# Cap first on SyncE's queue, and pair 7's normalization and the third weight unit's decoding moved to other places

## The chip, the cores and the metric

The kernel runs on one core of a Trainium2 chip. The core has five engines that run side by side, each its own list of instructions in a fixed order: TensorE (PE, with its weight loads as PEld), VectorE (DVE), ScalarE (ACT), GpSimd (POOL) and SyncE (SP), which only issues DMAs here. An instruction that needs another engine's result waits on a semaphore, and all that stands behind it on its own engine waits too. The metric is the device time of one execution in microseconds (us), as the median of several runs; less is better.

## The reference

Attention with capped scores, then a first feed-forward layer, then a gated one behind an RMS norm. All is float32.

```python
def _attn_ref(q, k, v, cap):                      # 2 x 12 heads, 448 tokens, 64 each
    scores = np.matmul(q, k.transpose(0, 1, 3, 2)) / np.sqrt(64)
    scores = cap * np.tanh(scores / cap)
    attn = np.exp(scores - np.max(scores, axis=-1, keepdims=True))
    attn = attn / (np.sum(attn, axis=-1, keepdims=True) + 1e-09)
    return np.matmul(attn, v)

x = attention, as (896, 768)
h = x @ w_in                                      # 768 x 2048
x = (h * (1.0 / (1.0 + np.exp(-1.702 * h)))) @ w_out
xn = x / np.sqrt(np.mean(x * x, axis=-1, keepdims=True) + 1e-06) * rms_g
g, val = xn @ w_gate, xn @ w_val                  # 768 x 1536 each
return (g * (1.0 / (1.0 + np.exp(-g))) * val) @ w_out2
```

## The kernel before

**Attention.** The 24 heads are taken as 12 pairs (p = 0 to 11), one head on each half of the 128 partitions. The 448 keys of a head are three chunks of 128 and one of 64. For each chunk PE multiplies keys with queries (scores, line 246, and scores_last, line 273), and ACT takes the tanh (line 292, line 262 for the first chunk of pair 0, in two halves) and then the exponential (line 295). The tanh needs `tsc`, 1 / (8 cap), which DVE works out from `capt` (lines 216 and 217), a DMA that spreads the one number cap over 128 partitions. The probabilities of chunks 0 and 1 lie in `pa`, those of chunk 2 and of the short chunk in `pb`. PE multiplies them with v (outputs, line 314), and copy_out moves the result to `z`.

**The sums below the fraction.** For pair p, add_two (line 333) adds chunks 0 and 1 on DVE into `ts`. add_third adds a further part: for pair 11 DVE adds chunk 2 (line 337), for pairs 1 to 9 two DMAs add the short chunk, for pairs 0 and 10 nothing is added. sums (line 356) then sums over the keys on PE by multiplying with ones: `ts`, then chunk 2 where it isn't in `ts`, then the short chunk where it isn't. DVE transposes the result, takes the reciprocal and transposes back (lines 361, 363 and 365, the last into `rs`), and spread (line 375) sends it out in four DMAs into `r`.

**The normalization.** norm(p) is three DVE instructions: norm_mul (line 378, z times r), norm_hi (line 383, x rounded to the form that TensorE multiplies fast) and norm_lo (line 390, what the rounding left). For pairs 10 and 11 norm_hi runs on ACT (line 385). NORMS tells which pairs are normalized in which step of the loop over p; at p = 12, the last step, pairs 8 and 9 have fixed places, and pairs 10 and 11 come behind the loop and behind the first feed-forward column.

**The weights.** Every weight is split into a high and a low part, so each product is three matmuls: high with x high (line 566), high with x low (line 567), low with x high (line 568). The weights come in units of 768 columns, as raw 32-bit words that are decoded: scale (ACT, line 129), shift, top and low (DVE, lines 133, 137 and 143), high_part (ACT, line 155) and low_part (DVE, line 160). Units 0 and 1 are decoded within the attention, as the table `plan` says. Unit 2 is decoded around the end of the attention, unit 3 behind it. low(w) is the last reader of a raw buffer; there are three, so unit 5 can be loaded only behind low(2).

**The first feed-forward columns.** A column is one unit times one part of the tokens: six groups (one for each 128 rows of x) of three matmuls. Part 0 is 384 tokens, which need pairs 0 to 5 alone, part 1 is 512, which need all. The columns come in the order (unit 0, part 0), (1, 0), (0, 1), (1, 1), (2, 1), (3, 1), (2, 0), (3, 0), (4, 0) and so on. Behind a column ACT takes the gate (line 592) and rounds it (line 595), and DVE takes what is left (line 598, into `g`).

**What sets the order.** The order on every engine is that in which the code is written (manual schedule). In the feed-forward part, tick() runs a column's products first, then the work that fell due, then the decoding of that place. The list `first` behind the first column decodes unit 2 as far as that has not been done, and then unit 3 and 4; an operation that has already run is skipped. Pair 11's steps (`norm_last`) fall due just behind the first column, and ahead of that column's own gate.

Of the kernel before, what the change touches and what calls it, by code (L numbers as in the profile page):

```python
# [12 lines left out]
ALU = mybir.AluOpType  # L13
# [4 lines left out]
def attn_moe_kernel(  # L18
# [14 lines left out]
    nc = tc.nc  # L33
# [10 lines left out]
    NPR = B * NP  # L44
# [4 lines left out]
    def f(ap):  # L49
        return ap.bitcast(F32)  # L50

    keep = ctx.enter_context(tc.tile_pool(name="keep", bufs=1))
    capt = keep.tile([128, 1], F32, name="capt")
# [108 lines left out]
    def run(op, w):  # L162
        if w < len(units) and (op, w) not in done:
            done.add((op, w))
            op(w)
# [8 lines left out]
    def attention():  # L174
        with ExitStack() as actx:
# [15 lines left out]
            xs, raws, vs, pa, pb, zt, nr, ts_ = {}, {}, {}, {}, {}, {}, {}, {}  # L191
# [15 lines left out]
            cuts = [slice(0, S), slice(64, 192), slice(192, XW - S), slice(0, 64)]  # L207
# [121 lines left out]
            LAST = range(1, NPR - 2)  # L329
# [5 lines left out]
            def add_third(p):  # L335
                if p == NPR - 1:
                    nc.vector.tensor_tensor(out=ts_[p], in0=ts_[p], in1=pb[p][:, 0:2], op=ALU.add)
                elif p in LAST:
                    for j in range(2):
                        nc.gpsimd.dma_start(  # L340
                            out=ts_[p][half[j], :, j * SH:(j + 1) * SH],
                            in_=pb[p][half[j], 2].rearrange("p (e s) -> p e s", e=2), accum_op=ALU.add,
                        )

            def sums(p):
                ps = ps_s.tile([128, 2, 512], F32, tag="s", name="s")[:, 0]
                streams = [ts_[p], *([] if p == NPR - 1 else [pb[p][:, 0:2]]), *([] if p in LAST else [None])]
                for n, some in enumerate(streams):
                    for e in range(2):
                        for j in range(2):  # L350
                            if some is None:
                                w, t = blk[:, 64 * j:64 * j + 32], pb[p][:, 2, e * SH:(e + 1) * SH]
                            else:
                                w, t = f(ones)[:, 0:32], some[:, e, j * SH:(j + 1) * SH]
                            r0 = 64 * j + 32 * e
                            nc.tensor.matmul(  # L356
                                out=ps[r0:r0 + 32, 0:SH], lhsT=w, rhs=t,
                                start=(n == 0), stop=(n == len(streams) - 1), skip_group_check=True,
                            )
                by_token = zrp.tile([128, SH // 32, 32], F32, tag="bt", name="bt", bufs=2)  # L360
                nc.vector.transpose(out=by_token.rearrange("p b t -> p (b t)"), in_=ps[:, 0:SH])
                few = zrp.tile([128, SH // 32], F32, tag="few", name="few", bufs=2)
                nc.vector.reciprocal(out=few, in_=by_token[:, :, 0])
                nr[p] = zrp.tile([128, SH], F32, tag="rs", name="rs", bufs=2)
                nc.vector.transpose(  # L365
                    out=nr[p], in_=few.rearrange("p (b o) -> p b o", o=1).to_broadcast([128, SH // 32, 32]),
                )
# [9 lines left out]
            def norm_mul(p):  # L377
                nc.vector.tensor_tensor(out=zt[p], in0=zt[p], in1=nr.pop(p), op=ALU.mult)

            def norm_hi(p):  # L380
                b, pp = divmod(p, NP)
                if p < NPR - 2:
                    nc.vector.tensor_copy(xA[0][:, pp, b * S:(b + 1) * S], zt[p])
                else:
                    nc.scalar.activation(out=xA[0][:, pp, b * S:(b + 1) * S], in_=zt[p], func=AF.Copy)

            def norm_lo(p):
                b, pp = divmod(p, NP)
                xx = slice(b * S, (b + 1) * S)
                nc.vector.tensor_tensor(  # L390
                    out=xA[1][:, pp, xx], in0=zt.pop(p), in1=f(xA[0][:, pp, xx]), op=ALU.subtract
                )

            def norm(p):
                for step in (norm_mul, norm_hi, norm_lo):
                    step(p)

            nc.vector.memset(f(xA[0][:, 0, 0:S]), 1.0)
            ts = first_kq()
            nc.scalar.dma_start(out=ts[0], in_=q[0])  # L400
            nc.scalar.dma_start(out=ts[2], in_=k[0, :, cuts[2]])
            nc.scalar.activation(out=tiny, in_=f(ones)[:, 0:1], func=AF.Tanh)
            nc.sync.dma_start(out=ts[1], in_=k[0, :, cuts[1]])
            nc.sync.dma_start(out=capt, in_=cap.rearrange("(o n) -> o n", o=1).to_broadcast([128, 1]))
            nc.sync.dma_start(out=ts[3], in_=k[0, :, cuts[3]])
            constants()
            load_kq(1)
# [22 lines left out]
            scale_by_cap()  # L430

            RAW = {1: 1, 3: 2, 4: 3, 10: 4}
            NORMS = {10: (4, 5), 11: (6, 7), 12: ()}

            for p in range(NPR + 1):
                load_kq(p + 3 if p < 2 else p + 4)
                load_v(p + 2)
                if p == 1:
                    load_kq(5)
                if p in RAW:  # L440
                    load_to(RAW[p])
                if p == 0:
                    first_scores()
                    scores(0, 1)
                    tanh(0, 1)
                    exp(pa[0][:, 0])
                    scores(0, 2)
                    tanh(0, 2)
                    scores_last(0)
                    tanh(0, NC)  # L450
                    exp(pa[0][:, 1])
                    exp(pb[0])
                    outputs(0, (0,))
                    split_kq(1)
                    for c in range(NC):
                        scores(1, c)
                    outputs(0, (1,))
                elif p < NPR:
                    for c in range(NC):
                        tanh(p, c)  # L460
                subtract = cast_kq(p + 2) if p + 2 < NPR else None
                for n in NORMS.get(p, (p - 6,) if p >= 6 else ()):
                    norm(n)
                decode(p, "b")
                if subtract:
                    subtract()
                decode(p, "c")
                if p >= 1:
                    if p == NPR:
                        add_third(p - 1)  # L470
                        sums(p - 2)
                        spread(p - 2)
                    if p < NPR:
                        outputs(p - 1, (NC,))
                        scores_last(p)
                        outputs(p - 1, range(NC) if p > 1 else (2,))
                    else:
                        outputs(p - 1)
                    if p < NPR:
                        copy_out(p - 1, "D")  # L480
                    done_ = p - 1 if p == 1 or p == NPR else p - 2
                    if done_ not in nr:
                        if p == NPR:
                            norm(8)
                        sums(done_)
                        if p == NPR:
                            copy_out(p - 1, "A")
                        spread(done_)
                        if p == NPR:
                            norm(9)  # L490
                if 1 <= p < NPR:
                    tanh(p, NC)
                    exp(pa[p])
                    exp(pb[p])
                if p < NPR:
                    add_two(p)
                    decode(p, "d")
                    if p < NPR - 1:
                        add_third(p)
                if p >= 1:  # L500
                    for c in range(NC):
                        scores(p + 1, c)
            norm_mul(NPR - 2)
            norm_hi(NPR - 2)
            run(shift, 2)
            norm_lo(NPR - 2)
            q_ = NPR - 1
            return lambda: norm_mul(q_), lambda: norm_hi(q_), lambda: run(low, 2), lambda: norm_lo(q_)

    def rest(*norm_last):  # L510
        with ExitStack() as fctx:
# [70 lines left out]
            def later(*fns):  # L582
                at(1, *[("D", True, fn) for fn in fns])
# [27 lines left out]
            for c in range(NC1):  # L611
# [15 lines left out]
                for n, (i, b) in enumerate(order):  # L627
                    last = ()
                    if c == 0 and n == 0:
                        later(lambda: run(top, 2), *norm_last)  # L630
                        last = (
                            lambda: [run(*some) for some in first], lambda: load_to(5), load_g,
                        )
                    ffn1(gA, u0 + i, i, b, slots[n], last)
# [245 lines left out]
```

## Time and profile before

| | us |
|---|---|
| median of 3 runs | 581.82 (581.73 to 582.35) |
| the profiled execution's own time | 581.33 |
| its span, first to last instruction | 579.5 |
| busy: PE, DVE, ACT, POOL | 573.1, 411.7, 274.0, 59.1 |

The span is what the trace shows; 1.83 us of the profiled execution lie around it. The profile has a page of sums, and the trace can be asked for the chain of work that ended last, for the instructions of a stretch in order of time (the timeline), for groups by line, and for the DMAs. In the timeline a row is start, duration, engine, line, operation, tiles, count; in brackets stands how long the engine had been idle and what ended that. Two instructions of one engine overlap a little, so that what one costs its engine is read from start to start.

### The profile page before, as it was taken

How to read it: one execution, taken by the hardware profiler on the slowest of the kernel's cores; microseconds unless marked ns; L12 is line 12 of the kernel's file. 1: busy time of each engine (PE TensorE's matmuls, PEld its weight loads, DVE VectorE, ACT ScalarE, POOL GpSimd, SP SyncE). 2: the span in 40 equal slices, each digit the busy share in tenths (PEclk: the TensorE clock that was granted, in tenths of full speed). 3: DMA queues.
4: the chain of work that ended last, by engine and by line, in shares of the span. 5: the costliest groups of instructions: out<-in, count | busy, mean ns of one | idle time of the engine just before them, and what ended most of it. 6: DMA issues, size and time to landing. Idle time of an engine off the chain costs nothing.

```text
span 579.5 us, 9374 instructions
## 1 busy us (share of the span) xinstructions
PE 573.1 (99%) x3842; PEld 493.4 (85%) x3842; DVE 411.7 (71%) x568; ACT 274.0 (47%) x369; POOL 59.1 (10%) x54
## 2 busy tenths in 40 slices
PE   8999999999999999999999999999999999999997
PEld 5566668988899998999998989889898998989887
DVE  3889997956653365656787999873787894778732
ACT  7999965755241355553444543442243431334300
POOL 0223300000000000000313013000222000222000
PEclk9999999999999999999999999999999999999999
DMA  8898643642624123233141514351232361232022
GB/s 282 243 225 219 113 116 91 200 146 92 198 67 152 55 81 127 96 123 118 56 156 63 165 59 160 109 164 54 58 110 106 110 217 55 63 108 102 1 92 100
DMA packets 60363, 70.31 MB, mean 121 GB/s; under 512 B 4128, under 2 KB 56480, under 8 KB 60320
## 3 DMA queue, kind: packets, MB, share of 16 engines
q1 hardware_dynamic: 57136, 66.91, 35.5%
q0 software_dynamic: 2592, 2.07, 3.0%
q10 hardware_dynamic: 592, 0.74, 0.4%
q8 instruction: 30, 0.49, 0.3%
q14 instruction: 13, 0.11, 0.1%
HBM read 62.13 MB, written 2.75 MB: 112 GB/s over the span
## 4 chain that ended last, share of the span: by engine, by line
PE 95%; ACT 3%; DMA 1%; issue 0%; DVE 0%; SPq 0%; ACTq 0%
PE b L568 28%; PE b L567 28%; PE b L566 28%; PE v L314 5%; PE s L246 3%; PE s L356 2%; ACT pa L292 1%; PE s L273 1%; ACT pb L292 1%; ACT pb L295 1%; DMA capt<-in_cap 1%; ACT pa L295 1%; ACT pa L262 0%; PE b L705 0%; DVE oacc L775 0%
## 5 line engine op out<-in xcount | busy, mean ns | idle before, releaser
L568 PE MATMUL b<-x,ring 128*128 128x384 f32 (+1 forms) x480 | 174.0, 363 | 0.0
L567 PE MATMUL b<-x,ring 128*128 128x384 f32 (+1 forms) x480 | 173.8, 362 | 0.0
L566 PE MATMUL b<-x,ring 128*128 128x384 f32 (+1 forms) x480 | 173.7, 362 | 0.0
L566 PEld LDWEIGHTS b<-x,ring 128*128 128x128 f32 x480 | 90.1, 188 | 9.8 <-DVE rs L365 0.4
L568 PEld LDWEIGHTS b<-x,ring 128*128 128x128 f32 x480 | 90.1, 188 | 9.6 <-DVE ring L160 0.3
L567 PEld LDWEIGHTS b<-x,ring 128*128 128x128 f32 x480 | 90.1, 188 | 9.6
L160 DVE TENSOR_TENSOR ring<-dec,ring 128x768 fp32r<-128x768 f32 x68 | 77.2, 1136 | 28.1 <-ACT ring L155 28.1
L568 PE MATMUL b<-g,ring 128*128 128x512 f32 (+1 forms) x192 | 69.7, 363 | 0.0
L567 PE MATMUL b<-g,ring 128*128 128x512 f32 (+1 forms) x192 | 69.6, 363 | 0.0
L566 PE MATMUL b<-g,ring 128*128 128x512 f32 (+1 forms) x192 | 69.5, 362 | 0.0
L155 ACT ACTIVATE ring<-dec 128x768 fp32r<-128x768 f32 x66 | 55.2, 837 | 29.8 <-DVE dec L143 24.5
L143 DVE SCALAR_TENSOR_TENSOR dec<-raw,dec 128x768 uint32<-128x768 uint32 x68 | 66.8, 983 | 1.2
L137 DVE SCALAR_TENSOR_TENSOR dec<-raw,dec 128x768 uint32<-128x768 uint32 x68 | 64.8, 953 | 1.0
L129 ACT ACTIVATE dec<-raw 128x768 f32<-128x768 f32 x66 | 59.8, 907 | 5.2 <-issue 2.5
L568 PE MATMUL b<-uA,ring 128*128 128x512 f32 (+1 forms) x144 | 52.1, 362 | 0.0
L567 PE MATMUL b<-uA,ring 128*128 128x512 f32 (+1 forms) x144 | 52.1, 362 | 0.0
L566 PE MATMUL b<-uA,ring 128*128 128x512 f32 (+1 forms) x144 | 52.1, 362 | 0.0
L737 POOL TENSOR_TENSOR a<-a,gg 128x512 f32<-128x512 f32 (+1 forms) x18 | 29.2, 1621 | 187.1 <-DVE gg L730 160.1
L598 DVE TENSOR_TENSOR g<-gg,g 128x384 fp32r<-128x384 f32 (+1 forms) x32 | 20.0, 624 | 39.7 <-ACT g L595 39.7
L740 ACT ACTIVATE uA<-a 128x512 fp32r<-128x512 f32 (+1 forms) x24 | 13.9, 580 | 70.3 <-POOL a L737 52.0
L133 DVE TENSOR_SCALAR dec<-dec 128x768 uint32<-128x768 uint32 x68 | 39.5, 581 | 0.0
L567 PEld LDWEIGHTS b<-g,ring 128*128 128x128 f32 x192 | 36.0, 188 | 3.9
(89 smaller groups left out, 665.5 us busy)
## 6 DMA issues: line engine op xcount, KB each, us to landing
raw<-in_moe_w_out SPq DMA_DIRECT2D x20, 768.0 KB, 4.2
raw<-in_moe_w_in SPq DMA_DIRECT2D x16, 768.0 KB, 4.5
raw<-in_moe_w_gate SPq DMA_DIRECT2D x12, 768.0 KB, 4.2
raw<-in_moe_w_val SPq DMA_DIRECT2D x12, 768.0 KB, 4.3
raw<-in_moe_w_out SPq DMA_DIRECT2D x8, 512.0 KB, 3.6
v<-in_v SPq DMA_DIRECT2D x11, 256.0 KB, 5.1
r<-rs SPq DMA_DIRECT2D x46, 56.0 KB, 3.1
kq<-in_k SPq DMA_DIRECT2D x11, 224.0 KB, 4.9
```

The source lines that it names most:

```text
L129: nc.scalar.activation(out=f(d), in_=f(hi), func=AF.Copy, scale=2.0 ** -112)
L133: nc.vector.tensor_scalar(out=d, in0=d, scalar1=3, scalar2=None, op0=ALU.logical_shift_left)
L137: nc.vector.scalar_tensor_tensor(out=d, in0=hi, scalar=0x80000000, in1=d, op0=ALU.bitwise_and, op1=ALU.bitwise_or)
L143: nc.vector.scalar_tensor_tensor(out=d, in0=lo, scalar=29, in1=d, op0=ALU.logical_shift_right, op1=ALU.bitwise_or)
L155: nc.scalar.activation(out=t[:, 0], in_=f(dec_t[w][0]), func=AF.Copy)
L160: nc.vector.tensor_tensor(out=t[:, 1], in0=f(d), in1=f(t[:, 0]), op=ALU.subtract)
L314: nc.tensor.matmul(out=ps[32 * n:32 * n + 32, j, 0:SH], lhsT=w[:, d0:d0 + 32], rhs=t, start=not before, stop=len(before) == NC, skip_group ...
L566: nc.tensor.matmul(out=wide(o, b), lhsT=w0, rhs=x0, start=first, stop=False)
L567: nc.tensor.matmul(out=wide(o, b), lhsT=w0, rhs=x1, start=False, stop=False)
L568: nc.tensor.matmul(out=wide(o, b), lhsT=w1, rhs=x0, start=False, stop=last)
L598: nc.vector.tensor_tensor(out=gA[1].at(i, hb), in0=gg[0], in1=f(gA[0].at(i, hb)), op=ALU.subtract)
L737: eng.tensor_tensor(out=t[0], in0=t[0], in1=t[1], op=ALU.mult)
```

## The change

Three things are moved or replaced, all in the attention and at its end:

- The DMA of cap is issued on SP ahead of that of the first chunk of keys (`ts[1]`, which the first scores multiply); before it came behind.
- Pair 10's chunk 2 is added into `ts` on DVE, as pair 11's was; its stream in sums falls away.
- Pair 7 is normalized at p = 12, where pair 8 was, rather than at p = 11; pair 8 goes behind the spread of pair 11, ahead of pair 9. shift, top and low of unit 2 lose their own places between the steps of pairs 10 and 11; they now run from the list `first`.

```diff
             def add_third(p):
                 if p == NPR - 1:
                     nc.vector.tensor_tensor(out=ts_[p], in0=ts_[p], in1=pb[p][:, 0:2], op=ALU.add)
+                elif p == NPR - 2:
+                    nc.vector.tensor_tensor(out=ts_[p], in0=ts_[p], in1=pb[p][:, 0:2], op=ALU.add)
                 elif p in LAST:
...
-                streams = [ts_[p], *([] if p == NPR - 1 else [pb[p][:, 0:2]]), *([] if p in LAST else [None])]
+                streams = [ts_[p], *([] if p >= NPR - 2 else [pb[p][:, 0:2]]), *([] if p in LAST else [None])]
...
             nc.scalar.dma_start(out=ts[0], in_=q[0])
+            nc.sync.dma_start(out=capt, in_=cap.rearrange("(o n) -> o n", o=1).to_broadcast([128, 1]))
+            nc.sync.dma_start(out=ts[1], in_=k[0, :, cuts[1]])
             nc.scalar.dma_start(out=ts[2], in_=k[0, :, cuts[2]])
             nc.scalar.activation(out=tiny, in_=f(ones)[:, 0:1], func=AF.Tanh)
-            nc.sync.dma_start(out=ts[1], in_=k[0, :, cuts[1]])
-            nc.sync.dma_start(out=capt, in_=cap.rearrange("(o n) -> o n", o=1).to_broadcast([128, 1]))
             nc.sync.dma_start(out=ts[3], in_=k[0, :, cuts[3]])
...
-            NORMS = {10: (4, 5), 11: (6, 7), 12: ()}
+            NORMS = {10: (4, 5), 11: (6,), 12: ()}
...
                         if p == NPR:
-                            norm(8)
+                            norm(7)
                         sums(done_)
                         if p == NPR:
                             copy_out(p - 1, "A")
                         spread(done_)
                         if p == NPR:
+                            norm(8)
                             norm(9)
...
             norm_mul(NPR - 2)
             norm_hi(NPR - 2)
-            run(shift, 2)
             norm_lo(NPR - 2)
             q_ = NPR - 1
-            return lambda: norm_mul(q_), lambda: norm_hi(q_), lambda: run(low, 2), lambda: norm_lo(q_)
+            return lambda: norm_mul(q_), lambda: norm_hi(q_), lambda: norm_lo(q_)
...
-                        later(lambda: run(top, 2), *norm_last)
+                        later(*norm_last)
```

SP's queue at the start of the program, before (`first1` is the first chunk of keys, `first3` the short one):

```order
L403 DMA first1_94<-in_k 128x128
L404 DMA capt_58<-in_cap 128x1
L405 DMA first3_96<-in_k 128x64
L197 DMA kq_107<-in_k 128x448
L198 DMA kq_107<-in_q 128x448
```

And now:

```order
L403 DMA capt_58<-in_cap 128x1
L404 DMA first1_94<-in_k 128x128
L407 DMA first3_96<-in_k 128x64
L197 DMA kq_107<-in_k 128x448
L198 DMA kq_107<-in_q 128x448
```

The two first DMAs have changed places; nothing else on this queue has moved.

VectorE at p = 10 and p = 11, before (`ts_1235` is pair 10's, `z_892` and `z_999` are pairs 6 and 7):

```order
L333 TENSOR_TENSOR ts_1235<-pa_1157 128x896
L378 TENSOR_TENSOR z_892<-z_892,r_1016 128x448
L383 CAST x0_64<-z_892 128x448
L390 TENSOR_TENSOR x1_65<-z_892,x0_64 128x448
L378 TENSOR_TENSOR z_999<-z_999,r_1122 128x448
L383 CAST x0_64<-z_999 128x448
L390 TENSOR_TENSOR x1_65<-z_999,x0_64 128x448
```

And now:

```order
L333 TENSOR_TENSOR ts_1235<-pa_1157 128x896
L339 TENSOR_TENSOR ts_1235<-ts_1235,pb_1160 128x896
L380 TENSOR_TENSOR z_892<-z_892,r_1016 128x448
L385 CAST x0_64<-z_892 128x448
L392 TENSOR_TENSOR x1_65<-z_892,x0_64 128x448
```

One addition has come in, and the three instructions of pair 7 have left.

VectorE at the end of the attention and behind it, before, from pair 9 on (`z_1210`, `z_1311` and `z_1416` are pairs 9, 10 and 11, `dec_1338` is unit 2):

```order
L378 TENSOR_TENSOR z_1210<-z_1210,r_1328 128x448
L383 CAST x0_64<-z_1210 128x448
L390 TENSOR_TENSOR x1_65<-z_1210,x0_64 128x448
L378 TENSOR_TENSOR z_1311<-z_1311,r_1360 128x448
L133 TENSOR_SCALAR dec_1338<-dec_1338 128x768
L390 TENSOR_TENSOR x1_65<-z_1311,x0_64 128x448
L137 SCALAR_TENSOR_TENSOR dec_1338<-raw_404,dec_1338 128x768
L378 TENSOR_TENSOR z_1416<-z_1416,r_1418 128x448
L143 SCALAR_TENSOR_TENSOR dec_1338<-raw_404,dec_1338 128x768
L390 TENSOR_TENSOR x1_65<-z_1416,x0_64 128x448
L598 TENSOR_TENSOR g1_1447<-gg_1473,g0_1445 128x384
L160 TENSOR_TENSOR ring_1479<-dec_1338,ring_1479 128x768
```

And now, from the last step of pair 8 (`z_1105`) and with pairs 10 and 11 as `z_1309` and `z_1410`, unit 2 as `dec_1336`:

```order
L392 TENSOR_TENSOR x1_65<-z_1105,x0_64 128x448
L380 TENSOR_TENSOR z_1210<-z_1210,r_1326 128x448
L385 CAST x0_64<-z_1210 128x448
L392 TENSOR_TENSOR x1_65<-z_1210,x0_64 128x448
L380 TENSOR_TENSOR z_1309<-z_1309,r_1354 128x448
L392 TENSOR_TENSOR x1_65<-z_1309,x0_64 128x448
L380 TENSOR_TENSOR z_1410<-z_1410,r_1412 128x448
L392 TENSOR_TENSOR x1_65<-z_1410,x0_64 128x448
L600 TENSOR_TENSOR g1_1443<-gg_1467,g0_1441 128x384
L133 TENSOR_SCALAR dec_1336<-dec_1336 128x768
L137 SCALAR_TENSOR_TENSOR dec_1336<-raw_404,dec_1336 128x768
L143 SCALAR_TENSOR_TENSOR dec_1336<-raw_404,dec_1336 128x768
```

Unit 2's three decoding steps stood between the steps of pairs 10 and 11; now all three stand behind pair 11 and behind the first column's `g`. Ahead of pair 9 there is one pair more. ScalarE's order is the same in both.

## Rows read from the trace of the kernel before

**Rows 1.** The page: granted clock by slices, and the chain by engine.

```profile
PEclk9999999999999999999999999999999999999999
...
PE 95%; ACT 3%; DMA 1%; issue 0%; DVE 0%; SPq 0%; ACTq 0%
```

**Rows 2.** The chain in order of time (start, us, what): two of its pieces.

```profile
24.73 0.91 ACT pa L292
...
78.33 1.89 PE s L356 x40
```

**Rows 3.** The timeline of the program's start, SP, PE, DVE and ACT.

```profile
0.76 0.38 SPq L403 DMA_DIRECT2D first<-in_k  x1
...
1.19 0.42 SPq L404 DMA_DIRECT2D capt<-in_cap  x1
...
4.08 1.83 PE L256 MATMUL s<-first,first 64*128 64x224 f32 x8
...
5.11 0.16 DVE L216 RECIPROCAL tsc<-capt 128x1 f32<-128x1 f32 x1 [3.62 <-DMA capt<-in_cap]
...
5.74 0.95 PE L246 MATMUL s<-first,first 64*128 64x448 f32 x4
...
6.73 1.01 ACT L292 ACTIVATE pa<-s,tsc 128x896 f32<-128x896 f32 x1
```

**Rows 4.** DMAs by line: queue, count, KB each, median us from issue to landing.

```profile
raw<-in_moe_w_in SPq DMA_DIRECT2D x16, 768.0 KB, 4.5
...
first<-in_k SPq DMA_DIRECT2D x1, 64.0 KB, 2.6
...
capt<-in_cap SPq DMA_DIRECT2D x1, 0.5 KB, 3.9
```

**Rows 5.** The timeline of VectorE, from pair 11's addition to unit 3's low part.

```profile
81.33 1.09 DVE L337 TENSOR_TENSOR ts<-ts,pb 128x896 f32<-128x896 f32 x1
...
85.96 0.58 DVE L378 TENSOR_TENSOR z<-z,r 128x448 f32<-128x448 f32 x1
...
87.00 0.63 DVE L390 TENSOR_TENSOR x<-z,x 128x448 fp32r<-128x448 f32 x1
87.55 0.62 DVE L378 TENSOR_TENSOR z<-z,r 128x448 f32<-128x448 f32 x1
...
88.81 0.63 DVE L390 TENSOR_TENSOR x<-z,x 128x448 fp32r<-128x448 f32 x1 [0.18 <-ACT x L385]
...
90.22 0.62 DVE L378 TENSOR_TENSOR z<-z,r 128x448 f32<-128x448 f32 x1
...
93.91 0.56 DVE L598 TENSOR_TENSOR g<-gg,g 128x384 fp32r<-128x384 f32 x1 [1.67 <-ACT g L595]
95.45 0.96 DVE L160 TENSOR_TENSOR ring<-dec,ring 128x768 fp32r<-128x768 f32 x1 [0.97 <-ACT ring L155]
96.32 0.55 DVE L133 TENSOR_SCALAR dec<-dec 128x768 uint32<-128x768 uint32 x1
...
97.90 0.96 DVE L143 SCALAR_TENSOR_TENSOR dec<-raw,dec 128x768 uint32<-128x768 uint32 x1
...
102.00 0.95 DVE L160 TENSOR_TENSOR ring<-dec,ring 128x768 fp32r<-128x768 f32 x1
```

**Rows 6.** The timeline of ScalarE in the same stretch.

```profile
90.94 0.58 ACT L385 ACTIVATE x<-z 128x448 fp32r<-128x448 f32 x1 [2.15 <-DVE z L378]
...
94.58 0.83 ACT L155 ACTIVATE ring<-dec 128x768 fp32r<-128x768 f32 x1
...
98.90 0.85 ACT L155 ACTIVATE ring<-dec 128x768 fp32r<-128x768 f32 x1 [2.68 <-DVE dec L143]
```

**Rows 7.** The timeline of TensorE: columns (2, 1) and (3, 1) as they start.

```profile
98.41 0.39 PE L566 MATMUL b<-x,ring 128*128 128x512 f32 x1
...
103.00 0.19 PEld L568 LDWEIGHTS b<-x,ring 128*128 128x128 f32 x1 [0.32 <-DVE ring L160]
```

**Rows 8.** Groups by line of the first 9 us: count, busy us, mean ns, idle before.

```profile
L417 PEld LDWEIGHTS s<-x,ones 128*128 128x128 f32 x6 | 1.8, 327 | 0.2
```

## The prediction

> **What bounds the kernel now.** First the page. The chain that ended last is PE for 95% of the span, and the granted clock stands at its full level in all 40 slices [rows 1]. So work on another engine counts only where PE waits for it. The chain in order of time shows two such places. Until about 25 us the chain is ACT, from the first tanh on, and then it is PE to the end; among PE's pieces are the sums over the keys at 78 us [rows 2]. The second place is found in the timeline behind the attention: in column (3, 1) PE sits idle before the first matmul with unit 3's low part, until VectorE's line 160 is done [rows 7]. That idle time is short, 0.32 us of the weight load, most of it usual; what matters is that it is there at all. Unit 3's low part arrives just when it is needed, and has no slack. So VectorE's list between 82 and 103 us, which elsewhere runs far ahead, is as critical there as PE. I read it from start to start [rows 5], with ScalarE's steps that it waits for [rows 6].
>
> **The change part by part. Cap first.** Cap goes out at 0.76 us where it went at 1.19, so it lands some 0.43 us earlier, and the first tanh no longer waits so long for line 216 [rows 3]. But ACT's next tanh, that of the second chunk, starts at 6.73, and the scores that it reads are PE's four instructions from 5.74 to 6.69 [rows 3]. Those don't wait for cap. So the most that this part can give is 6.73 - 6.69 = 0.04 us; the rest becomes idle time of ACT one instruction later. The price is that the first chunk of keys now goes out at 1.19, and PE needs it at 4.08, with nothing else of use to do. Landing as fast as before (2.6 us), it comes at 3.8 and costs nothing; taking as long as cap did in that same second place (3.9 us), it comes at 5.1 and costs 1.0 us [rows 3, 4]. From there ACT works without a gap until it hands the chain to PE at 25 us [rows 2], so a delay would stay to the end. The bounds are -0.04 and +1.0. I take +0.2, near the end that the chunk's own row gives, since the same bytes in the same pieces are moved.
>
> The Trainium skill ("DMA: Bandwidth & Descriptors", Specifications) says that pieces under 512 bytes are not moved at the line rate, which speaks against putting 128 pieces of four bytes in front; the trace agrees so far as cap, with 0.5 KB, took longer than a chunk of 64 KB [rows 4]. By that rule alone the term would be at its upper end, 1.0.
>
> **Pair 10's chunk 2.** sums(9) and sums(10) are five streams in 1.89 us, 0.38 each [rows 2]. One falls away, so PE is 0.38 us earlier from there on. The addition costs VectorE 1.09 us, by pair 11's row [rows 5]. It stands at p = 10 to 11, and pair 7's three steps leave the same stretch (a norm is 87.55 - 85.96 = 1.59 us [rows 5]), so VectorE is earlier there and not later, and nothing else waits. Without that cover the addition would push the copy of pair 10's output, and with it the outputs of pair 11 on PE, by up to 1.09.
>
> **Pair 7 at p = 12, unit 2 behind everything.** Up to pair 11's transposes nothing changes: pair 7's 1.59 us stand where pair 8's stood. From 85.96 there are two norms (8 and 9) where there was one, and behind them the steps of 10 and 11 without the decoding that used to fill their waits for ACT. Step by step, each distance from the rows of before:
>
> - norm_mul(10): 87.55 + 1.59 = 89.14 [rows 5].
> - norm_lo(10) follows 88.81 - 87.55 = 1.26 later: 90.40. VectorE sits idle for the rounding on ACT, which the shift of unit 2 used to fill.
> - norm_mul(11) another 87.55 - 87.00 = 0.55 later: 90.95. ACT's rounding of pair 11 90.94 - 90.22 = 0.72 later: 91.67, where it was 90.94 [rows 5, 6].
> - ACT's table load, gate and rounding and then VectorE's line 598 came 93.91 - 90.94 = 2.97 behind that: 94.64.
> - Only then the decoding of unit 2: shift at most 0.56 later, 95.20; low 97.90 - 96.32 = 1.58 behind shift, 96.78.
> - ACT's high part of unit 2 must now wait for low, as unit 3's did: 98.90 - 97.90 = 1.00 later, 97.78. VectorE's low part 95.45 - 94.58 = 0.87 later: 98.65, where it was 95.45. That is +3.20.
> - From unit 2's low part to unit 3's the lists of VectorE and ACT are those of before: 102.00 - 95.45 = 6.55 later, 105.20. PE's load came 1.00 behind its start: 106.20 where it was 103.00.
>
> So PE, which would reach that load 0.38 us earlier than before, gets it 3.20 later; the 0.38 is lost in the wait. The wait falls in three pieces. Column (2, 1), which started at 98.41 [rows 7] and could now start at 98.03, waits for unit 2's high part (97.78 plus 0.83 us) and then for its low part (98.65 + 1.00 = 99.65), about 0.6 and 0.8 us. Column (3, 1) waits the rest, about 2.4. Pairs 10 and 11 themselves come in time: PE needs the last of them in the sixth group of column (0, 1). A matmul is 0.23 us there (20 starts from 98.41 to 103.00 [rows 7]) and a column 4.1, so (0, 1) starts two columns ahead of 98.03, at 89.8, and asks for pair 11 at 93.2; its high part is done at 91.67 + 0.58 = 92.25 and its low part about 0.6 later.
>
> Two more things hang on the late low(2). Unit 5's load is issued behind it, at about 97.7, and lands at 102.2 by the median of 4.5 us [rows 4]; ACT asks for it behind unit 3's high part, at about 102.9, so 0.7 us are left. And unit 4 is needed only four columns behind the start of (2, 1), some 14 us later (two of 4.1 and two of three quarters of that); nothing else gets late, and nothing gives the time back, since PE has no idle time behind this to shrink.
>
> **The sum** against the profiled execution: 581.33 + 3.2 (unit 3's low part, with the 0.38 inside it) + 0.2 (first chunk) = 584.7. The median of the runs is 0.49 above that execution, so the forecast is 585.2.
>
> **Rivals.** *The first chunk is late.* It lands as cap did in second place; the second term is 1.0 and not 0.2, and the time 586.0. For it speaks cap's row, against it that chunk's own [rows 4]. 18%.
>
> *The clock falls in the wait.* PE sits idle about 2.4 us of some 8, which it never does within the products of before. At the program's start a weight load takes 327 ns [rows 8] against 190 at 103 us [rows 7], though the clock row reads full there too [rows 1], so PE has a slow pace of 1.2 GHz beside its 2.4. If it fell to that, the price lies between nothing and half the slow stretch of the start (first matmul to about 5.6 us, 4.5 us long): 2.3 us, for a time up to 587.5. 10%. The Trainium skill ("TensorE: Matmul & The Clock Gate", HAM oscillation) tells of kernels whose waits cost them the full clock each time; no row here shows a fall after a short wait.
>
> *The waits overlap better.* Only pair 7's 1.59 us come to VectorE's list, and the new waits for ACT are absorbed in the old ones (1.67 and 0.97 us [rows 5]). Then unit 3 is 1.6 late: 583.4. Against it: the old waits lie behind ACT's steps, which move as well. 10%.
>
> *Faster.* The decoding is hidden after all, and the shorter sums and the earlier cap show: -0.38 and -0.43, for 581.0. It needs unit 3's low part done by 102.6, 3.5 us sooner than I have it, and cap to count in full. Against it stands that PE already waited at 103.00 [rows 7]. 5%.
>
> **The numbers.** The forecast has 57%, the rivals 18, 10, 10 and 5. The range from 583.3 to 587.0 leaves out the fast case, a part of the overlapping one and the worst of the clock. About 0.2% (1.2 us) is what a measurement of this kernel can tell from no change, so the bounds are 580.7 and 583.0: faster 2%, same 6%, slower 92%.
>
> **What would show it.** In the new trace PE's idle time before unit 2's high and low part and before unit 3's low part, together over 3 us, released by ACT and by line 160; VectorE idle ahead of norm_lo(10), norm_lo(11) and line 598; the high part of unit 2 on ACT at about 97.8. For the start: the first scores at 4.1 (no loss) or 5.1, and the second chunk's tanh at 6.7 or later. If line 160 of unit 3 starts by 102 us, or PE's chain shows no wait there, the prediction is wrong at its main term.

## The result, and the profile after

The changed kernel takes 586.47 us (median of 5 runs, 586.40 to 588.07) where the kernel before took 581.73 beside it. The ratio is 1.0093, with a 95% interval from 1.0080 to 1.0107: 5.4 us slower (4.7 to 6.2). The ratio is that of the means; the medians are 4.7 us apart, because the runs of the changed kernel lie at two times, three near 586.4 and two near 588.0. The profiled execution is one of the longer ones (588.07 us, span 586.3, against 581.33 and 579.5 before).

The chain of the changed kernel in order of time (start, us, what) shows at once two stretches that the chain of before did not have, a DMA of keys with PE behind it at the start, and VectorE and ACT from 82 to 108 us:

```profile
1.20 4.09 DMA first<-in_k
5.42 1.86 PE s L256 x8
7.29 1.51 PE s L246 x4
...
26.83 0.91 ACT pa L292
...
83.43 1.09 DVE ts L337
...
99.81 0.85 ACT ring L155
100.68 0.96 DVE ring L160
...
107.31 0.88 DVE ring L160
108.23 0.79 PE b L570
```

ACT's tanh that stood at 24.73 [rows 2] stands at 26.83: 2.10 us had been lost by then. VectorE's addition for pair 11, at 81.33 before [rows 5], stands at 83.43: still 2.10. So nothing was lost or gained between the start and the end of the attention.

The start, in the timeline of the changed kernel, against [rows 3]:

```profile
0.75 0.39 SPq L403 DMA_DIRECT2D capt<-in_cap  x1
...
1.20 0.42 SPq L404 DMA_DIRECT2D first<-in_k  x1
...
4.68 0.17 DVE L216 RECIPROCAL tsc<-capt 128x1 f32<-128x1 f32 x1 [3.19 <-DMA capt<-in_cap]
...
5.42 1.86 PE L256 MATMUL s<-first,first 64*128 64x224 f32 x8 [1.28 <-DMA first<-in_k]
...
7.05 2.77 PE L246 MATMUL s<-first,first 64*128 64x448 f32 x8
...
8.82 1.01 ACT L292 ACTIVATE pa<-s,tsc 128x896 f32<-128x896 f32 x1 [0.86 <-PE s L246]
```

Cap is earlier by 0.43 us, as it was meant to be, and ACT has no use for it, since the first scores are not there. PE starts them at 5.42 instead of 4.08 (1.34 later), and then needs 7.05 to about 8.8 for the second chunk's, where it needed 5.74 to 6.69: 0.8 us more for the same four instructions. The tanh behind them is at 8.82 instead of 6.73, which is the 2.1 us.

VectorE of the changed kernel, against [rows 5], and ACT, against [rows 6]:

```profile
91.27 0.62 DVE L380 TENSOR_TENSOR z<-z,r 128x448 f32<-128x448 f32 x1
92.53 0.62 DVE L392 TENSOR_TENSOR x<-z,x 128x448 fp32r<-128x448 f32 x1 [0.64 <-ACT x L387]
93.08 0.62 DVE L380 TENSOR_TENSOR z<-z,r 128x448 f32<-128x448 f32 x1
94.40 0.62 DVE L392 TENSOR_TENSOR x<-z,x 128x448 fp32r<-128x448 f32 x1 [0.70 <-ACT x L387]
96.76 0.56 DVE L600 TENSOR_TENSOR g<-gg,g 128x384 fp32r<-128x384 f32 x1 [1.73 <-ACT g L597]
97.23 0.56 DVE L133 TENSOR_SCALAR dec<-dec 128x768 uint32<-128x768 uint32 x1
...
100.68 0.96 DVE L160 TENSOR_TENSOR ring<-dec,ring 128x768 fp32r<-128x768 f32 x1 [0.91 <-ACT ring L155]
...
107.22 0.95 DVE L160 TENSOR_TENSOR ring<-dec,ring 128x768 fp32r<-128x768 f32 x1
```

```profile
99.81 0.84 ACT L155 ACTIVATE ring<-dec 128x768 fp32r<-128x768 f32 x1 [2.29 <-DVE dec L143]
```

Five waits stand in brackets. Three of them are new or longer: 0.64 and 0.70 us for ACT's rounding of pairs 10 and 11 (0.18 and nothing before), which decoding used to fill, and ACT's 2.29 us ahead of unit 2's high part, which now waits for VectorE's decoding. That high part begins at 99.81, which without the start's 2.10 is 97.71. Unit 3's low part starts at 107.22 instead of 102.00. Of these 5.22 us, 2.10 are the start's, and 3.12 were lost here.

TensorE of the changed kernel, against [rows 7]. It waits for unit 2's high part, for its low part and for unit 3's low part:

```profile
100.70 0.50 PE L568 MATMUL b<-x,ring 128*128 128x512 f32 x1 [0.41 <-ACT ring L155]
...
101.70 0.50 PE L570 MATMUL b<-x,ring 128*128 128x512 f32 x1 [0.26 <-DVE ring L160]
...
108.23 0.79 PE L570 MATMUL b<-x,ring 128*128 128x512 f32 x1 [2.15 <-DVE ring L160]
108.82 0.63 PE L568 MATMUL b<-x,ring 128*128 128x512 f32 x1
109.25 0.63 PE L569 MATMUL b<-x,ring 128*128 128x512 f32 x1
...
111.72 0.39 PE L569 MATMUL b<-x,ring 128*128 128x512 f32 x1
111.95 0.39 PE L570 MATMUL b<-x,ring 128*128 128x512 f32 x1
```

From 108.82 the starts are 0.43 us apart, from 111.72 on 0.23. The stretches of the same execution (length, busy us of PE, PEld, DVE, ACT and POOL with counts, then the granted clock, DMA share, GB/s) say why:

```profile
106.00:107.00 1.00, 0.07 (x1) 0.00 (x0) 0.81 (x2) 0.97 (x3) 0.00 (x0) 1.00 1.01 330
107.00:108.00 1.00, 0.00 (x0) 0.00 (x0) 1.00 (x2) 0.97 (x3) 0.00 (x0) 1.00 1.09 355
108.00:109.00 1.00, 0.77 (x2) 0.68 (x3) 1.00 (x3) 0.89 (x2) 0.00 (x0) 0.60 1.19 273
109.00:110.00 1.00, 1.00 (x4) 0.81 (x3) 1.00 (x2) 1.00 (x2) 0.00 (x0) 0.50 1.06 378
110.00:111.00 1.00, 1.00 (x4) 0.71 (x4) 0.96 (x2) 0.97 (x3) 0.00 (x0) 0.50 0.49 166
111.00:112.00 1.00, 1.00 (x5) 0.83 (x4) 1.00 (x3) 0.97 (x3) 0.00 (x0) 0.69 0.00 1
```

After two idle microseconds the granted clock is 0.50 of full, 1.2 GHz, for some 3.4 us, which costs about 1.6 us, the distance between the two times of the runs. The sum of the three is 2.10 + 3.12 + 1.6 = 6.8, the difference of the spans (586.3 - 579.5). The runs at 586.4 have no such fall (mean granted clock 1.000, against 0.997 in those at 588), and 2.10 + 3.12 = 5.2 is what they show against the span of before.

### The profile page after: what moved, and what is told of

It reads as the page before. It is cut to its first block, busy times and chain, and to the rows that moved or that the text cites. A ratio compares the mean times of both kernels' runs of the same rounds, so it can differ in the third digit from the quotient of the medians.

```text
span 586.3 us, 9360 instructions
## 1 busy us (share of the span) xinstructions
PE 575.8 (98%) x3834; PEld 495.5 (85%) x3834; DVE 413.5 (71%) x569; ACT 274.2 (47%) x369; POOL 59.1 (10%) x54
## 4 chain that ended last, share of the span: by engine, by line
PE 91%; ACT 3%; DVE 3%; issue 1%; DMA 1%; SPq 0%; DVEq 0%; ACTq 0%
PE b L570 27%; PE b L569 27%; PE b L568 27%; PE v L314 5%; PE s L246 3%; PE s L358 1%; PE s L273 1%; DMA first<-in_k 1%; ACT pb L295 1%; ACT pa L295 1%; ACT pa L292 1%; ACT pb L292 0%; DVE z L380 0%; DVE dec L137 0%; DVE dec L143 0%
```

## The experiments

Two theories went in. A: the start costs 2.1 us by itself, through the late chunk and PE's slow pace behind it, and the lists of VectorE and ACT behind the attention cost 3.1. B, as the forecast had it: the start is worth 0.2 to 1.0, and the rest was lost elsewhere.

### Cap first, alone

```diff
 kernel before
+dma capt (SP)
 dma ts[1] (SP)
-dma capt (SP)
```

> The kernel before with the cap's DMA ahead of the first chunk of keys, and nothing else. Theory A (the start cost more than the forecast had): the first tanh of the second chunk comes 2.1 us later, at about 8.8 instead of 6.73 us, because the chunk lands near 5.3 us and PE's first two sets of scores run at its slow pace; all of it stays, so about 583.8 us. Theory B (the forecast): the start costs 0.2 us, or 1.0 if the chunk lands as cap did, so 581.9 to 582.7, and the other 1.1 to 1.9 us of the changed kernel come from somewhere in the attention.

Measured: 583.37 us, ratio 1.0031 (1.0021 to 1.0042). The timeline of this kernel has PE's first scores and the second chunk's tanh where the changed kernel has them:

```profile
5.41 1.86 PE L256 MATMUL s<-first,first 64*128 64x224 f32 x8 [1.26 <-DMA first<-in_k]
...
8.81 1.01 ACT L292 ACTIVATE pa<-s,tsc 128x896 f32<-128x896 f32 x1 [0.86 <-PE s L246]
```

Theory A holds: this one swap of two DMAs costs 2.1 us in the trace (span 581.6 against 579.5). By the ratio it is 1.8 us (1.2 to 2.4): the trace of before has one of the earliest second tanhs of its kind, as the next run shows.

### All but the cap

```diff
 changed kernel
-dma capt (SP)
 dma ts[1] (SP)
+dma capt (SP)
```

> The changed kernel with the old order of the two DMAs. Theory A: the start is as in the kernel before (second chunk's tanh at 6.73), and unit 3's low part on VectorE is 3.1 us later than there, at about 105.1 us, for 584.8 us where the clock holds and up to 1.6 more where it falls in the wait. Theory B: the start has little part in it, so the time stays near that of the changed kernel, 586 us or more.

Measured: 585.05 us, ratio 1.0062 (1.0044 to 1.0081). The five runs are 584.35, 584.70 and 585.05 at full mean clock, and 585.96 and 586.70 at 0.997. In the trace VectorE's addition for pair 11 is at 81.91 and unit 3's low part at 105.69, 23.78 us behind it, where it was 102.00 - 81.33 = 20.67 before: 3.11 lost. The two parts add up, within their intervals: 0.31% and 0.62% against the 0.93% of the whole.

The expectation on the start was only nearly met: the second chunk's tanh is at 7.31 here, not at 6.73. PE's scores for it, unchanged from the kernel before, took longer in this execution. Other kernels below, with the same start, show the same spread.

### Only the decoding moved, and only the sums and pair 7

```diff
 kernel before
-            run(shift, 2)                  # between norm_hi(10) and norm_lo(10)
...
-    later(lambda: run(top, 2), *norm_last)
+    later(*norm_last)                      # and no run(low, 2) among norm_last
```

> The kernel before with shift, top and low of unit 2 taken from between the steps of pairs 10 and 11, so that they run from the list behind the first column, and nothing else. By the distances of the rows of before: norm_mul(11) at 89.36, the table load and gate behind it, unit 2's low part at 97.0 instead of 95.45 and unit 3's at 103.6 instead of 102.0, so +1.55 us, 583.3; if pair 11's reciprocals have not landed by 89.4, up to 0.5 more. The rival, that PE's list has slack there for it, gives 581.7.

Measured: 583.39 us, ratio 1.0027 (1.0017 to 1.0037). From pair 11's addition to unit 3's low part it is 104.03 - 81.86 = 22.17 us: +1.50. PE waits 1.41 us for it.

```diff
 changed kernel, cap behind ts[1] as before
+            run(shift, 2)                  # back between the steps of pair 10
...
+    later(lambda: run(top, 2), *norm_last) # and run(low, 2) back in norm_last
```

> The changed kernel with the old order of the two DMAs and with unit 2's three steps back in their old places; what is left is pair 10's addition on VectorE and pair 7 normalized at p = 12. VectorE's list is 1.59 us longer between pair 9 and unit 3's low part, which comes at 103.6 instead of 102.0: +1.6 us, 583.3, with the 0.38 us of the shorter sums lost in PE's wait. The rival, that the shorter sums show, gives 581.3. With the run where only the decoding is moved, the two should add up to the 3.1 us that the changed kernel shows behind the attention.

Measured: 582.92 us, ratio 1.0026 (1.0017 to 1.0035). The same distance is 103.60 - 81.32 = 22.28: +1.61. PE waits twice, in column (0, 1) for pair 11's low part and in column (3, 1) for unit 3's, and the timeline names what for:

```profile
93.92 0.50 PE L570 MATMUL b<-x,ring 128*128 128x512 f32 x1 [0.23 <-DVE x L392]
...
104.61 0.50 PE L571 MATMUL b<-x,ring 128*128 128x512 f32 x1 [1.31 <-DVE ring L160]
```

So 1.50 and 1.61 make the 3.11 of the run before. PE's 0.38 us were won (column (0, 0) starts at 83.47 in this trace, at 83.86 before) and lost again in these waits. The first wait is not in the trace of the changed kernel: with the decoding out of its way, pair 11 is normalized sooner there.

### Filling PE's wait

```diff
 changed kernel, in ffn1
+if u == 3 and b == 1:
+    for _ in range(10):
+        matmul(o, lhsT=ones, rhs=x high of pair 0, start=True, stop=True)
```

> The changed kernel with ten more matmuls of ones with 512 columns, ahead of column (3, 1) and into its bank, which the column's first matmul then overwrites. They take 2.27 us at 0.23 each and lie in PE's wait for unit 3's low part, so they cost nothing by themselves. Theory A (the idle time is what brings the clock down): the granted clock stays full in every run, and all runs lie at the lower of the changed kernel's two times, 586.4, none at 588. Theory B (the clock falls for another reason, or the two times have another cause): some runs at 588 as before.

Measured: 586.22 us (586.16, 586.21, 586.22, 586.25 and 586.67), ratio 1.0082 (1.0068 to 1.0095). No run is at 588. The timeline shows the filler in the wait, and the real matmul with unit 3's low part as early as without it:

```profile
105.18 2.50 PE L591 MATMUL b<-x,ones 128*128 128x512 f32 x10
107.52 0.40 PE L568 MATMUL b<-x,ring 128*128 128x512 f32 x1
107.75 0.39 PE L569 MATMUL b<-x,ring 128*128 128x512 f32 x1
107.98 0.47 PE L570 MATMUL b<-x,ring 128*128 128x512 f32 x1
```

From 108.29 on the starts are 0.23 us apart; there is no slow stretch. Five runs are not many: the two kernels with this wait fell in two of five runs each, and at that rate five runs without a fall come by chance about once in 13 times. One of the five (586.67) shows a mean granted clock of 0.95 with hardly any loss of time, which stays unexplained. For theory A speaks also that the wait is where the clock fell in the trace, and that the two kernels above with a shorter wait there (1.41 and 1.31 us) show no mean clock under 0.999 in 19 runs. So the idle time as the cause is likely by these runs, but not proved.

### How the start's loss divides: the late chunk and PE's pace

```diff
 kernel before, cap first
-    WARM = 6
+    WARM = 10
```

> The kernel before with the cap's DMA first, as in the run that changes nothing else, and with ten warm-up matmuls of 448 columns instead of six. The four more take about 1.5 us at the slow pace, so PE works until the first chunk of keys lands near 5.3 us. Theory A (PE's 1.3 us of idle time there put off its full pace): the first scores start at about 5.5 at full pace, the second chunk's tanh comes at about 7.2 instead of 8.8, and of the 2.0 us that cap first costs some 1.5 come back: 581.9. Theory B (the late chunk alone is what costs): the tanh stays at 8.8 and the time at 583.4.

Measured: 582.09 us, ratio 1.0009 (1.0000 to 1.0017): of the 0.31% that cap first costs, 0.22 are back. The timeline, against the start above:

```profile
1.55 3.79 PE L417 MATMUL s<-x,ones 128*128 128x448 f32 x10
...
5.27 1.03 PE L256 MATMUL s<-first,first 64*128 64x224 f32 x8
...
6.13 1.67 PE L246 MATMUL s<-first,first 64*128 64x448 f32 x8
...
7.10 1.01 ACT L292 ACTIVATE pa<-s,tsc 128x896 f32<-128x896 f32 x1
```

The scores start at nearly the same time as with cap first alone (5.27 and 5.41), but take 1.03 us instead of 1.86, and the tanh is at 7.10 instead of 8.81. So keeping PE at work through the 1.3 us in which it stood idle brings it to its full pace by the first scores, and gives back 1.7 us in the trace (1.3 by the ratio).

That isn't to say that 1.7 of the 2.1 us came from the pace. In the kernel before the first set of scores ran at the slow pace too (1.83 us [rows 3]), so some 0.8 of the 1.7 is a gain that it didn't have either. Against the kernel before, cap first costs 1.33 us by the later start of the first scores (5.41 and 4.08) and some 0.75 by the second set, which was at full pace before and is at the slow one now.

### What made the chunk late: its place or cap's DMA

```diff
 kernel before
+dma ts[3] (SP)
 dma ts[1] (SP)
-dma capt (SP)
-dma ts[3] (SP)
+dma capt (SP)
```

> The kernel before with the short chunk of keys (32 KB, rows of 256 bytes) first on SP's queue, the first chunk of keys second and cap third. Theory A (cap's small pieces hold up what comes behind them): the first chunk lands in time for the first scores at 4.1 us, only cap is late by 0.5 us or more, and the second chunk's tanh is at 7.2 at the most: +0.5 us, 581.9. Theory B (second place alone costs over a microsecond): the first scores start near 5.4 as with cap first, and the time is 583.4.

Measured: 582.63 us, ratio 1.0020 (1.0012 to 1.0029). PE's first scores start at 4.08, as before. The DMAs of this kernel (KB, us from issue to landing):

```profile
first<-in_q ACTq DMA_DIRECT2D x1, 224.0 KB, 2.8
first<-in_k ACTq DMA_DIRECT2D x1, 128.0 KB, 3.0
first<-in_k SPq DMA_DIRECT2D x1, 64.0 KB, 2.6
first<-in_k SPq DMA_DIRECT2D x1, 32.0 KB, 2.3
capt<-in_cap SPq DMA_DIRECT2D x1, 0.5 KB, 4.5
```

And the same of the changed kernel:

```profile
first<-in_q ACTq DMA_DIRECT2D x1, 224.0 KB, 4.3
first<-in_k ACTq DMA_DIRECT2D x1, 128.0 KB, 4.5
first<-in_k SPq DMA_DIRECT2D x1, 64.0 KB, 4.1
first<-in_k SPq DMA_DIRECT2D x1, 32.0 KB, 4.2
capt<-in_cap SPq DMA_DIRECT2D x1, 0.5 KB, 3.9
```

The chunk of 64 KB, second on the queue both times and issued at 1.19 and 1.20, takes 2.6 us behind 32 KB of keys and 4.1 behind half a KB of cap. With cap behind them, the four loads of queries and keys land within 3.0 us; with cap ahead, none in under 4.1, not even on ACT's queue. The six traces with cap second agree: what went out ahead of it took 2.5 to 2.9 us, what went out beside or behind it 3.2 to 4.3. So it isn't the place but cap's DMA. What it is in this DMA, the pieces of four bytes or the one address that is read for all 128 partitions, no run separates; pieces of 256 bytes, those of the short chunk, do not do it. The size of the gain was missed: cap itself came at about 6.2 us, later than thought, and the tanh of the second chunk at 7.72, not 7.2. Two of the 11 runs (583.35 and 583.40) show a mean granted clock of 0.997, though VectorE's and ACT's lists behind the attention are those of the kernel before and PE has no wait in brackets there in the trace; where the clock fell in these two, no trace shows.

### A version that takes the sums and fills the waits

```diff
 changed kernel, cap behind ts[1], shift, top and low of unit 2 back among pairs 10 and 11
-(12, "b"): [(scale, 2)],
+(12, "b"): [(scale, 2), (scale, 3)],
...
-later(lambda: run(top, 2), *norm_last)
+later(lambda: run(top, 2), *norm_last, lambda: run(high_part, 2), lambda: run(shift, 3),
+      lambda: run(low_part, 2), lambda: run(top, 3), lambda: run(low, 3))
```

> Pair 10's addition on VectorE and pair 7 at p = 12 as in the changed kernel, the old order of the two DMAs, unit 2's shift, top and low back between the steps of pairs 10 and 11, and besides: the scale of unit 3 on ACT behind that of unit 2, the high part of unit 2 on ACT ahead of the table load, and on VectorE unit 2's low part and unit 3's shift, top and low ahead of the first column's g. Theory: VectorE's idle time ahead of g and of unit 2's low part (1.67 and 0.97 us before) is filled, unit 3's low part comes before 102 us, PE no longer waits there, and the 0.38 us of the shorter sums show: 0.4 to 0.5 us less than before, 580.9. The rival, that the moved steps come late again and PE waits, gives 581.4 to 583.

Measured: 581.46 us, ratio 0.9999 (0.9990 to 1.0008), no difference. Unit 3's low part is at 100.54 now, and PE does not wait for it. But it waits earlier, in column (0, 1), for pair 11's low part, as it did with only the sums and pair 7 changed:

```profile
94.08 0.50 PE L570 MATMUL b<-x,ring 128*128 128x512 f32 x1 [0.24 <-DVE x L392]
```

```diff
-    *norm_last with run(low, 2) ahead of norm_lo(11), behind run(top, 2)
+    *norm_last with run(top, 2) ahead of norm_lo(11), then run(low, 2)
```

> As the run with all decoding moved forward, but with unit 2's top behind norm_mul(11) and its low behind norm_lo(11), so that VectorE reaches pair 11's low part 0.87 us sooner and PE's 0.24 us of waiting for it in column (0, 1) fall away. Theory: PE does not wait at all behind the attention, the 0.38 us of the shorter sums and the 0.1 at unit 3 show in full, and the time is 581.1, 0.4 below the kernel before. The rival, that another wait takes its place or the start's own spread (0.6 us) hides it, gives 581.3 to 581.7, no difference that can be told.

Measured: 580.80 us, ratio 0.9985 (0.9976 to 0.9994), 0.9 us (0.3 to 1.4) faster than the kernel before beside it (581.85). In its trace PE has no wait in brackets from 83 to 125 us, and its span is 579.3, though its start was one of the slower (second chunk's tanh at 7.08).

## Why the prediction was wrong

**Where PE would wait, and for what: right.** The step-by-step sum gave unit 3's low part 3.20 us later; it was 3.12, and the parts 1.50 and 1.61 against 1.55 and 1.59 worked out for them ahead of their runs. The waits fell on unit 2's high and low part and unit 3's low part, as listed. From start to start they cost 0.56, 0.42 and 2.31 us, where 0.6, 0.8 and 2.4 were forecast; the second had been put too high. PE's 0.38 us were lost in the wait. The rival in which the new waits are absorbed in the old ones, and the one in which the decoding stays hidden, are both excluded by these rows.

**That cap's gain ends one instruction later: right.** In the changed kernel it never came to bear, because the scores were not there. But in the trace without cap first, line 216 happened to start at 4.33 instead of 5.11, and ACT then sat idle for 0.69 us ahead of the second chunk's tanh, until PE's scores were done.

**The term of the first chunk: wrong in size.** It was put at 0.2, with bounds of -0.04 and 1.0, and measured 2.10. Two steps failed. The chunk's own row of 2.6 us was taken as the nearest, though that row is of a chunk with nothing in front of it; cap's row, in the same second place, was nearer, and even that was passed (4.1). That put the first scores 1.34 us later, beyond the bound of 1.0. And the bound carried the delay of the chunk over to the tanh one to one. The rows showed PE at its slow pace in the warm-up just ahead of the first scores (load of 327 ns [rows 8]), but the prediction used that row only for the wait 100 us later. After 1.28 us of idle time PE was still at that pace in the second set of scores, which before ran at the full one; that is the other 0.75 us or so of the 2.10. The run with the longer warm-up shows that the pace can be had back by keeping PE at work.

The sentence from the Trainium skill ("DMA: Bandwidth & Descriptors", Specifications), that pieces under 512 bytes are not moved at the line rate, pointed to the upper end. It does not explain the runs by itself: the short chunk moves in pieces of 256 bytes, and behind it the first chunk still landed in 2.6 us.

**The clock: a rival, and it came beside the forecast, not in its place.** It was given 10% and up to 2.3 us; the clock fell in two of five runs of the changed kernel and two of five of the one without cap first, and cost 1.6 us. A wait that a sum forecasts at 2.4 us should have carried a share of that price. The Trainium skill ("TensorE: Matmul & The Clock Gate", HAM oscillation) tells of a kernel that lost the full clock at every one of its waits for data. The row at 109 us agrees in kind, but here the clock fell in some executions only.

With the measured terms the sum is 581.33 + 3.12 + 2.10 = 586.55, and the three runs in which the clock held lie at 586.40 to 586.47. The forecast of 585.2 was short of them by 1.3 us, not by the start's other 1.9: the 0.49 that it added to get from the profiled execution to the median made up for part. The median, 586.47, lies within the forecast's range; the 5.4 us of the ratio, which counts the two runs at 588, put the time at 587.1, just above it. The range's upper end added the rivals one at a time, though the late chunk and the clock do not exclude each other.

## What to carry to other kernels

When a step is taken out of a place where it stood between two waits, its cost is the waits that it filled, not its own time. Walking the list from start to start gave that cost here to a tenth of a microsecond. Where idle time is forecast or a transfer that PE needs at its start is moved, price PE's pace as well as the delay, and work that keeps PE busy through the wait is the cheapest test of it. A DMA of few bytes need not be a small one: the half KB of cap, spread over 128 partitions, belonged behind what was needed first.

## What was not expected of the hardware

- A broadcast of one number to 128 partitions (0.5 KB) took 3.1 to 4.5 us from issue to landing over all traces and in every place on the queue, and with it first the DMAs that ran beside it took about 1.5 us longer, on ACT's queue too (224 KB: 2.8 us with cap third, 4.3 with cap first).
- PE's pace at the program's start is not to be seen in the granted clock, which reads 1.00 in the first 25 us of both kernels, but in its loads: 334 ns in the scores at line 246 of the changed kernel, 188 later. The second chunk's tanh came at 6.73, 6.93, 7.08, 7.25 and 7.31 us in traces of kernels with the same start; when PE gets to its full pace differs from one execution to the next by over half a microsecond.
- An idle stretch of PE of 2.15 us, in one column of a program that otherwise keeps it busy, was followed by half the granted clock in the changed kernel's trace (0.50), while one of 2.14 us in the same place, in the trace without cap first, was not (1.00).
